# One-bank PSUM tiles, and loads ordered around DMA transposes, in an attention-and-mixer kernel

## The chip, the cores and the metric

The kernel runs on one core of one Trainium2 chip. The metric is device time in microseconds (us) of one execution. The profile also gives the span from the first to the last instruction.

## The reference, cut to what matters

```python
# q, k, v: [8 batches, 8 heads, 576 tokens, 64]; omega: [128, 64]
def phi(x):                       # random features, x scaled by 64 ** -0.25
    h = x @ omega.T - sum(x * x) / 2
    return exp(h - max(h)) / sqrt(128)
q_p, k_p = phi(q), phi(k)                  # [8, 8, 576, 128]
kv, z = k_p.T @ v, sum(k_p over tokens)    # per head
x = (q_p @ kv) / (q_p @ z + 1e-6)          # [8, 576, 512] over all heads
# token mixing, then channel mixing
u = x + (relu(x.T @ w_tok1) @ w_tok2).T    # 576 -> 256 -> 576
out = u + relu(u @ w_ch1) @ w_ch2          # 512 -> 1536 -> 512
```

What is constant in a token of q cancels in the division, so the kernel takes no maximum and no square sum for q. For k it divides by a maximum of the exponentials themselves, over the features of each token.

## The kernel before, in words

**Tiling.** Each batch b has 512 main tokens and a tail of 64; the tails of two batches share one 128-row tile. Attention goes by pairs of heads, `hp` = 0 to 3. Per pair: `kp` and `qp` multiply k and q, both with the head dimension on the partitions, by omega (lines 528 and 546); ACT takes the exponentials; DVE takes the maxima (`km`, line 558); Pool multiplies v by their reciprocals (`vs_`, line 567); `kv` (line 577) sums over the tokens; ACT copies it to SBUF; `num` (line 602) multiplies by the q features; DVE divides (`num_out`, lines 617 and 618) and writes x. The tails go through `kt`, `qt` and `vbd` first, once in a batch. Then token mixing (`token_mix`; the first batch in `token_mix_halves`) gives u, and channel mixing (`channel_mix`) gives the output: 48 matmuls on line 740 with a ReLU on ACT (line 746), 48 on line 755 and a sum on DVE (line 761). A ninth channel mixing (index B = 8) does all the tails, from `uTt`.

**How operands get their layout.** k and q of batches 0 and 1 are loaded with the tokens on the partitions and transposed on TensorE (`load_nat`, `transposes`, `tail_transposes`). For batches 2 to 7, `load_transposed` makes two steps per operand: a DMA from Pool casts fp32 to fp16 into a scratch in DRAM (line 335), and a DMA transpose from SP (line 341) brings it back as `qT` or `kT`. Pool then copies the tail's columns of `kT` to `ktt` (line 472). u of batches 1 to 7 is transposed into `uT` the same way from SP (line 659), and the tails' `ut` into `uTt` (line 729). SP also issues the stores and the loads of v's tails; Pool issues every load that casts, in one fixed order (`issued`).

**Order of work.** The order on each engine is planned ahead in Python. A job has an engine, an estimated cost, a key (smaller goes first), jobs that it depends on, buffers that it takes and buffers that it gives back. `Planner.run` picks, for each engine, the job that can start first by these estimates, ties by key. The instructions come out in that order and each engine runs its own list in order. The waits between engines are semaphores that the framework adds from which tile is read and written, so what really happens can differ from the estimates, and an instruction that waits holds up all behind it on its engine. While TensorE would be idle early on, `warm` puts in matmuls of zeros (line 799).

**PSUM.** It has eight banks, each 512 fp32 per partition. Before, they are four tiles of two banks:

```python
banks = [pspool.tile([P, 2, 512], FP32, name=f"bank{i}") for i in range(4)]
```

A job takes one bank (`width` 1) or an aligned pair (`width` 2: kt, qt, kp, qp, num). For single banks `find` has a preference: among those free by the estimates, one whose sibling in the same tile is in use goes first.

Of the kernel before, what the change touches and what calls it, by code (L numbers as in the profile page):

```python
# [26 lines left out]
class Planner:  # L27
# [25 lines left out]
    def find(self, tag, width=1):  # L53

        free = self.places[tag]
        best = None
        for i in range(0, len(free), width):
            at = max(free[i : i + width])
            tie = 0.0
            if width == 1 and tag == "bank":  # L60
                tie = -1.0 if free[i ^ 1] == math.inf else 0.0
            if at < math.inf and (best is None or (at > self.now, tie if at <= self.now else 0.0, at) < best[2]):
                best = (i, at, (at > self.now, tie if at <= self.now else 0.0, at))
        return best
# [3 lines left out]
    def run(self):  # L68
        at = {"PE": 0.0, "ACT": 0.0, "DVE": 0.0, "POOL": 0.0, "SP": 0.0}
# [5 lines left out]
        while any(waiting.values()):  # L75
            choice = None
            for eng, jobs in waiting.items():
                ready = []
                for j in jobs:
# [13 lines left out]
                    for tag, name, width in j.take:  # L93
                        if (tag, name) in self.held:
                            continue
                        got = self.find(tag, width)
                        if got is None:
                            ok = False
                            break
                        t = max(t, got[1])  # L100
# [30 lines left out]
            for tag, name, width in j.take:  # L131
                if (tag, name) in self.held:
                    continue
                i = self.find(tag, width)[0]
                for k in range(width):
                    self.places[tag][i + k] = math.inf
                self.held[tag, name] = (i, width)
# [13 lines left out]
            for g in j.give:  # L151
                self.left[g] -= 1
                self.freed[g] = max(self.freed.get(g, 0.0), j.end)
                if self.left[g] == 0:
                    i, width = self.held[g]
                    for k in range(width):
                        self.places[g[0]][i + k] = self.freed[g]
        return max(at.values())

    def place(self, tag, name):  # L160
        return self.held[tag, name][0]
# [3 lines left out]
def kernel(  # L165
# [12 lines left out]
    nc = tc.nc  # L178
# [27 lines left out]
    def ring(n, shape, dt, name):  # L206
# [3 lines left out]
             "kvsb": 3, "ktt": 2, "x": 3, "r1": 3, "u": 3, "uT": 3, "r3": 2, "o": 4, "bank": 8}  # L210
# [3 lines left out]
    banks = [pspool.tile([P, 2, 512], FP32, name=f"bank{i}") for i in range(4)]  # L214
# [3 lines left out]
    ident16 = sb([P, P], FP16, "ident16")  # L218
    zeros = sb([P, SM], FP16, "zeros")
# [38 lines left out]
    for b, t in ((0, t_r3[0]), (1, t_r3[1])):  # L258
        for i, w in enumerate("qk"):
            nat[w, b] = flat(t)[:, i * H * 256 : (i + 1) * H * 256].rearrange("p (h e) -> p h e", h=H)  # L260
        nat["t", b] = flat(t)[:, 2 * H * 256 : 2 * H * 256 + H * 2 * D].rearrange("p (h e) -> p h e", h=H)
# [7 lines left out]
    def bank(name):  # L269
        i = place("bank", name)  # L270
        return banks[i // 2][:, i % 2, :]
# [4 lines left out]
    def pair(name):  # L276
        return banks[place("bank", name) // 2]
# [20 lines left out]
    def load_nat(b, w, h0, h1, key, deps=()):  # L298
# [5 lines left out]
        job = dma("POOL", key, (h1 - h0) * 0.36, go, deps)  # L304
# [3 lines left out]
    def load_nat_tail(b, w, key, deps=()):  # L308
        o = 0 if w == "q" else RT
        def go():  # L310
            nc.gpsimd.dma_start(
                out=nat["t", b][o : o + RT], in_=src[w][b, :, SM:S, :].rearrange("h (r e) d -> r h (e d)", e=2)
            )
        ld[w + "t", b] = dma("POOL", key, 0.4, go, deps)

    def load_v(b, key, deps=(), h0=0, h1=H):
        def main():
            nc.gpsimd.dma_start(out=t_v[place("v", b)][:, h0:h1, :], in_=v[b, h0:h1, 0:SM, :].rearrange("h (p j) d -> p h (j d)", j=NJ))
        job = dma("POOL", key, 0.37 * (h1 - h0), main, deps, take=[("v", b, 1)], cost=0.5 + 0.05 * (h1 - h0))
# [3 lines left out]
    def load_v_tail(b, key, deps=()):  # L323
# [6 lines left out]
        ld["vt", b] = dma("SP", key, 0.5, tails, take=[("vt", b, 1)], deps=deps, cost=0.9)  # L330

    def load_transposed(b, key, deps=()):
        for n, w in enumerate("qk"):
            def cast(w=w):
# [3 lines left out]
                )  # L338
            def back(w=w):
                t = (t_qT if w == "q" else t_kT)[place(w + "T", b)]  # L340
                nc.sync.dma_start_transpose(out=t.unsqueeze(1), in_=scratch[w, b])
            c = dma("POOL", key + 0.01 * n, 2.9, cast, deps, cost=0.55)
            ld[w + "T", b] = dma("SP", key + 0.2 + 0.01 * n, 2.2, back, deps=[c], take=[(w + "T", b, 1)], cost=3.0)
# [11 lines left out]
    load_v_tail(0, -8.8)  # L355
    load_nat_tail(0, "k", -8.8)
    load_nat(0, "k", 4, 8, -8.7)
    load_nat_tail(0, "q", -8.6)
    load_nat(0, "q", 0, 4, -8.5)
    load_nat(0, "q", 4, 8, -8.4)  # L360
    load_v(0, -8.3, (), 0, 4)
    load_v(0, -8.2, (), 4, 8)

# [33 lines left out]
    for i in range(2):  # L397
# [7 lines left out]
                deps=[j_om16, j_ident], take=[("bank", "om", 1)])  # L405
# [9 lines left out]
    def transposes(b, w, h0, h1, key, on_act=False):  # L415
# [13 lines left out]
        take = [("bank", name, 1)]  # L429
        take.append((w + "T", b, 1))  # L430
# [5 lines left out]
    def tail_transposes(b, w, key):  # L436
        name, o = ("tt", b, w), 0 if w == "q" else RT
        def go():
            ps = bank16(name)
            for h in range(H):  # L440
                nc.tensor.transpose(ps[:, h * RT : (h + 1) * RT], nat["t", b][o : o + RT, h, :], ident16[o : o + RT, o : o + RT])
        def out_():
            ps = bank16(name)[:, 0 : H * RT].rearrange("p (h c) -> p h c", h=H)
            if w == "k":
                nc.vector.tensor_copy(out=t_ktt[place("ktt", b)].rearrange("p (h r) -> p h r", h=H), in_=ps)
            else:
                nc.vector.tensor_copy(out=rows_of(b, "q")[:, :, R:RA], in_=ps)
        t = add("PE", mm(8, 32), key, go, deps=[ld[w + "t", b], j_ident], take=[("bank", name, 1), ("ktt", b, 1) if w == "k" else ("qT", b, 1)], rows=True)
# [7 lines left out]
    def attention(b, key, step):  # L456
# [13 lines left out]
        if dma_in:  # L470
            def ktt():
                nc.gpsimd.tensor_copy(out=t_ktt[place("ktt", b)].rearrange("p (h r) -> p h r", h=H), in_=rows_of(b, "k")[:, :, R:RA])
            j_ktt = add("POOL", 0.5, key, ktt, deps=[ld["kT", b]], take=[("ktt", b, 1)], give=[("kT", b)])
# [7 lines left out]
        j_kt = add("PE", mm(2, P), key, kt, deps=[j_ktt, j_omT], take=[("bank", n_kt, 2), ("kpt", b, 1)], give=[("ktt", b)], rows=True)  # L481
        def kt_exp():
            exp(t_kpt[place("kpt", b)].rearrange("p g e m -> p e g m"), pair(n_kt)[:, :, 0 : 2 * M].rearrange("p e (g m) -> p e g m", g=2))
        j_kte = add("ACT", 0.5, key, kt_exp, deps=[j_kt], take=[("kpt", b, 1)], give=[("bank", n_kt)])
# [13 lines left out]
        j_ktm = add("DVE", 1.0, key + 0.01, kt_max, deps=[j_kte, j_mask], take=[("vbd", b, 1)])  # L498
# [16 lines left out]
        j_qt = add("PE", mm(1, 256), key + 0.1 * step, qt, deps=[src_of("q"), j_omT], take=[("bank", n_qt, 2), ("qpt", b, 1)], rows=True)  # L515
# [3 lines left out]
        j_qte = add("ACT", 0.5, key + 0.1 * step, qt_exp, deps=[j_qt, j_pads], take=[("qpt", b, 1)], give=[("bank", n_qt)])  # L519

        last_x = []
        for hp in range(NU):
# [5 lines left out]
            def kp(n_k=n_k, hh=hh):  # L528
                ps = pair(n_k)
                for i in range(2):  # L530
                    m = main("k", hh[i])
                    for r in range(2):
                        for e in range(2):
                            c = (2 * i + r) * M
                            nc.tensor.matmul(ps[:, e, c : c + M], m[half[e], r, :], omT[half[e]], start=True, stop=True)  # L535
            j_k = add("PE", mm(4, P), g, kp, deps=[src_of("k", hh[0]), src_of("k", hh[1]), j_omT], take=[("bank", n_k, 2), ("kp", (b, hp), 1)], rows=True,
# [4 lines left out]
            for e in range(2):  # L541
                def kp_exp(e=e, n_k=n_k, hp=hp):
                    exp(t_kp[place("kp", (b, hp))][:, :, e, :], pair(n_k)[:, e, :].rearrange("p (c m) -> p c m", c=4))
                je.append(add("ACT", 0.5, g, kp_exp, deps=[j_k], take=[("kp", (b, hp), 1)], give=[("bank", n_k)]))

            def qp(n_q=n_q, hp=hp):
                ps, t = pair(n_q), rows_of(b, "q")
                for e in range(2):
                    nc.tensor.matmul(ps[:, e, :], omT[half[e]], t[half[e], 2 * hp : 2 * hp + 2, 0:R], start=True, stop=True)  # L549
            j_q = add("PE", mm(1, 512), gq, qp, deps=[src_of("q", hh[0]), src_of("q", hh[1]), j_omT], take=[("bank", n_q, 2), ("qp", (b, hp), 1)], rows=True,  # L550
                      give=[("qT", b)])
            jq = []
            for e in range(2):
                def qp_exp(e=e, n_q=n_q, hp=hp):
                    exp(t_qp[place("qp", (b, hp))][:, e, :], pair(n_q)[:, e, :])
                jq.append(add("ACT", 0.5, gq, qp_exp, deps=[j_q], take=[("qp", (b, hp), 1)], give=[("bank", n_q)]))
# [8 lines left out]
            j_m = add("DVE", 1.42, g + 0.3 * step * (b > 0), km, deps=je, take=[("vs", (b, hp), 1)])  # L565
# [27 lines left out]
            j_kv = add("PE", mm(8, 65) + mm(2, 130), gv, kv, deps=[j_v, j_vbd, *je], take=[("bank", n_kv, 1), ("kvsb", (b, hp), 1)],  # L593
# [6 lines left out]
            j_kvo = add("ACT", 0.25, gv, kv_out, deps=[j_kv], take=[("kvsb", (b, hp), 1)], give=[("bank", n_kv)])  # L600
# [11 lines left out]
            j_n = add("PE", mm(10, 65), gv + 0.1 * step, num, deps=[j_kvo, j_qte, *jq], take=[("bank", n_n, 2), ("x", b, 1)],  # L612
# [11 lines left out]
            last_x.append(add("DVE", 1.04, gv + 0.1 * step, num_out, deps=[j_n], take=[("x", b, 1)], give=[("bank", n_n)]))  # L624
        return last_x, j_start

    def token_mix(b, key, step, jx):
        jr = []
        for tb in range(NT):
# [6 lines left out]
            j1 = add("PE", mm(5, 512), key + step * tb * 0.2, t1, deps=[*jx, j_w1, *j_w1t], take=[("bank", n, 1), ("r1", b, 1)])  # L636
            def relu(tb=tb, n=n):
# [3 lines left out]
                else:  # L641
                    nc.vector.tensor_relu(out=o, in_=bank(n))  # L642
            jr.append(add("ACT" if tb == 0 else "DVE", 0.5 if tb == 0 else 0.69, key + step * tb * 0.2, relu, deps=[j1],
                          take=[("r1", b, 1)], give=[("bank", n)]))
        ju = []
        for j in range(NJ):
# [5 lines left out]
            j2 = add("PE", mm(2, 512), key + step * (0.5 + 0.1 * j), t2, deps=[*jr, j_w2], take=[("bank", n, 1), ("u", b, 1)], give=[("r1", b)])  # L652
# [179 lines left out]
```

The softmax here doesn't subtract the row's maximum and nothing guards it: scores larger than these inputs give would overflow.

## Time and profile before

| What | Value |
|---|---|
| Times of three runs | 349.41, 357.22, 370.53 us |
| Median | 357.22 us |
| Profiled run | 348.81 us, span 347.1 us |
| Mean granted TensorE clock in it | 0.977 |
| PE (matmuls) busy | 296.5 us, 85% of the span |
| DVE, ACT, Pool busy | 148.3, 151.7, 79.9 us |
| Line 755, line 740 on PE | 105.0 us in 432 matmuls, 94.6 us in 384 |
| DMA | 39.58 MB, mean 114 GB/s |
| Queue that Pool feeds, queue that SP feeds | 32.9% and 30.7% of 16 engines' span |

The strips of the profile cut the span in 40 slices of 8.7 us; each digit is a busy share in tenths, and PEclk is the clock granted to TensorE in tenths of full speed. A wait line tells which engine and line waited, for which engine and line, then the total, the number of times and the longest, in us. A timeline line has start and length in us, engine, line, operation, what it writes and reads, how many are merged, and in brackets the idle time before it and what ended that. SPq is SP's queue: a DMA's line there lasts as long as issuing it holds the queue, not until the data has landed. Matmuls overlap in a pipeline, so the mean duration of one (383 ns for 512 columns) is longer than the 216 ns that one takes in a dense row.

### The profile page before, as it was taken

The numbers are of one execution on the slowest core, as the hardware profiler recorded it, in microseconds if no ns is written. First come the engines' busy times: TensorE is split into PE (matmuls) and PEld (weight loads), VectorE is DVE, ScalarE is ACT, GpSimd is POOL, SyncE is SP. The second block draws the span as 40 slices with busy tenths as digits, with TensorE's granted clock in tenths as the row PEclk, the third lists the DMA queues.
The fourth block names the chain that finished last, engine by engine and source line by source line (L and its number), as shares of the span: only waits on it lengthen the run. The fifth ranks groups of instructions, "written<-read, shape, count | busy, mean of one in ns | idle before, by whom it ended". The sixth has DMA issues, their size and how long they took to land.

```text
span 347.1 us, 5467 instructions
## 1 busy us (share of the span) xinstructions
PE 296.5 (85%) x2196; PEld 145.5 (42%) x2196; DVE 148.3 (43%) x302; ACT 151.7 (44%) x300; POOL 79.9 (23%) x92
## 2 busy tenths in 40 slices
PE   7788898089978968798889988989899979899993
PEld 3466354034534424344434433444344434344441
DVE  2874852228527552066345624563445323302011
ACT  1954872054654345425463456336643630150520
POOL 8692430015305170111330303021202100000000
PEclk9999999769999989999999999999999999999998
DMA  7999999993999999666694410411032003301104
GB/s 104 197 177 196 222 202 114 58 201 121 210 163 183 122 256 225 98 150 155 143 170 109 112 45 0 93 60 48 0 75 78 33 0 91 108 0 60 62 20 101
DMA packets 69849, 39.58 MB, mean 114 GB/s; under 512 B 47424, under 2 KB 64704, under 8 KB 69440
## 3 DMA queue, kind: packets, MB, share of 16 engines
q0 software_dynamic: 17408, 17.40, 32.9%
q1 hardware_dynamic: 52416, 21.83, 30.7%
q8 instruction: 17, 0.28, 0.3%
q14 instruction: 8, 0.07, 0.0%
HBM read 35.91 MB, written 16.52 MB: 151 GB/s over the span
## 4 chain that ended last, share of the span: by engine, by line
PE 59%; DMA 19%; DVE 11%; ACT 6%; issue 2%; POOL 2%; DVEq 0%; ACTq 0%
PE bank L740 24%; PE bank L755 22%; DMA qT<-q 7%; DMA q<-in_q_dram 5%; DMA uT<-u 4%; ACT r L746 3%; PE bank L634 3%; DVE u L654 3%; DMA wc<-in_moe_w_ch_dram 2%; PE bank L799 2%; DVE o L761 2%; PE bank L651 2%; DVE km L562 1%; POOL vs L569 1%; DVE mx L561 1%
## 5 line engine op out<-in xcount | busy, mean ns | idle before, releaser
L755 PE MATMUL bank<-wc,r 128*128 128x512 f16 x432 | 105.0, 383 | 9.8 <-DVE ut L727 3.7
L740 PE MATMUL bank<-uT,wc 128*128 128x512 f16 x384 | 94.6, 384 | 18.4 <-ACT r L746 9.3
L746 ACT ACTIVATE r<-bank 128x512 f16<-128x512 f32 x108 | 61.3, 600 | 96.2 <-PE bank L740 45.8
L740 PEld LDWEIGHTS <-wc 128*128 128x128 f16 x432 | 41.1, 98 | 65.4 <-issue 22.5
L755 PEld LDWEIGHTS <-r 128*128 128x128 f16 x432 | 40.7, 98 | 59.6 <-issue 18.1
L569 POOL TENSOR_TENSOR vs<-v,vs 128x512 f16<-128x512 f16 x32 | 34.1, 1070 | 108.5 <-DVE rc L617 53.3
L761 DVE TENSOR_TENSOR o<-u,bank 128x512 f32<-128x512 f16 x32 | 21.8, 685 | 56.4 <-PE bank L755 40.2
L452 ACT ACTIVATE kp<-bank 128x512 f16<-128x512 f32 x64 | 34.5, 610 | 20.9 <-PE bank L535 20.9
L452 ACT ACTIVATE qp<-bank 128x512 f16<-128x512 f32 x64 | 35.7, 628 | 14.0 <-PE bank L549 13.9
L618 DVE TENSOR_TENSOR x<-bank,rc 128x640 f16<-128x640 f32 x32 | 26.4, 824 | 1.1
L617 DVE RECIPROCAL rc<-bank 128x10 f32<-128x10 f32 x32 | 6.7, 208 | 43.9 <-PE bank L611 41.2
L596 ACT CAST kvsb<-bank 128x130 f16<-128x130 f32 x32 | 8.7, 283 | 35.7 <-DVE o L761 19.0
L654 DVE TENSOR_TENSOR u<-x,bank 128x512 f16<-128x512 f16 x28 | 17.9, 682 | 14.2 <-PE bank L651 11.8
L501 POOL TENSOR_TENSOR vbd<-vt,vbd 128x1024 f16<-128x1024 f32 x8 | 15.6, 1949 | 33.9 <-DVE vbd L492 33.9
L562 DVE TENSOR_REDUCE km<-mx 128x8 f16<-128x512 f16 x32 | 21.9, 686 | 1.1
L561 DVE TENSOR_TENSOR mx<-kp 128x512 f16<-128x512 f16 x32 | 17.1, 534 | 10.9 <-ACT kp L452 10.8
L549 PE MATMUL bank<-qT,omT 64*128 64x512 f16 x64 | 12.4, 386 | 10.2 <-DMA qT<-q 9.5
L582 PEld LDWEIGHTS <-kp 128*128 128x128 f16 x256 | 11.8, 98 | 8.8 <-issue 2.0
L609 PEld LDWEIGHTS <-qp 128*128 128x128 f16 x256 | 12.5, 98 | 6.4 <-issue 0.9
L634 PE MATMUL bank<-x,w1m 128*128 128x512 f16 x56 | 14.4, 379 | 0.0
L651 PE MATMUL bank<-r,w 128*128 128x512 f16 x56 | 14.4, 379 | 0.0
L642 DVE TENSOR_SCALAR r<-bank 128x512 f16<-128x512 f32 x7 | 4.8, 691 | 22.0 <-PE bank L740 11.8
(84 smaller groups left out, 249.1 us busy)
## 6 DMA issues: line engine op xcount, KB each, us to landing
out_dram<-o SPq DMA_DIRECT2D x32, 256.0 KB, 2.3
v<-in_v_dram POOLq DMA_DIRECT2D x7, 512.0 KB, 11.5
q<-in_q_dram POOLq DMA_DIRECT2D x6, 576.0 KB, 7.1
k<-in_k_dram POOLq DMA_DIRECT2D x6, 576.0 KB, 10.2
wc<-in_moe_w_ch_dram POOLq DMA_DIRECT2D x4, 768.0 KB, 13.9
vt<-in_v_dram SPq DMA_DIRECT2D x16, 64.0 KB
out_dram<-o SPq DMA_DIRECT2D x8, 128.0 KB, 2.3
r<-in_q_dram POOLq DMA_DIRECT2D x2, 256.0 KB, 6.7
```

Of the source, the lines that this page charges most:

```text
L452: nc.scalar.activation(out=out, in_=in_, func=AF.Exp, bias=0.0, scale=c_scale)
L561: nc.vector.tensor_tensor(out=tmp, in0=kpv[:, :, 0 : M // 2], in1=kpv[:, :, M // 2 : M], op=ALU.max)
L562: nc.vector.reduce_max(out=mx, in_=tmp, axis=AX.X)
L569: nc.gpsimd.tensor_tensor(out=vs[:, :, 0:D], in0=t_v[place("v", b)][:, hh[0] : hh[0] + 2, :].rearrange("p h (j d) -> p (h j) d", d=D), in1 ...
L618: nc.vector.tensor_tensor(out=t_x[place("x", b)][:, :, hp * 2 * D : (hp + 1) * 2 * D].rearrange("p j (i d) -> p i j d", i=2), in0=ps[:, :, ...
L634: nc.tensor.matmul(ps, w1m[:, j, tb * P : (tb + 1) * P], x[:, j, :], start=(j == 0), stop=False)
L651: nc.tensor.matmul(ps, w2[:, tb, 0:SM].rearrange("p (c j) -> p j c", j=NJ)[:, j, :], r1[:, tb, :], start=(tb == 0), stop=(tb == NT - 1))
L654: nc.vector.tensor_tensor(out=t_u[place("u", b)][:, j, :], in0=t_x[place("x", b)][:, j, :], in1=bank(n), op=ALU.add)
L740: nc.tensor.matmul(ps, wc1[:, db, cb * P : (cb + 1) * P], moving(db), start=(db == 0), stop=(db == ND - 1))
L746: nc.scalar.activation(out=t_r3[place("r3", c)][:, cb, :], in_=bank(n), func=AF.Relu)
L755: nc.tensor.matmul(ps, r3[:, cb, j * P : (j + 1) * P], wc2[:, cb, :], start=(cb == 0), stop=(cb == NCB - 1))
L761: nc.vector.tensor_tensor(out=t_o[place("o", (c, j))], in0=uu, in1=bank(n), op=ALU.add)
```

## The change

It has three parts, as its short description says: PSUM tiles of one bank instead of two; casts kept apart from DMA transposes by copies on Pool that read the transposes; tails in 4 KB rows.

- PSUM becomes six tiles of one bank and one tile of two. kp and qp take two single banks each and give each back by itself; kt, qt and num share the one pair. `find` has no preference for a sibling any more: of the banks free by the estimates it takes the one that has been free longest.
- The casts of q and k of a batch are queued one after the other, and each of the two transposes depends on both. The ktt copy moves into `load_transposed`; v of the batch depends on it. A new one-column copy on Pool, `touch`, reads the end of `uT` of batch b (1 to 5) into `junk`, and the casts of batch b + 2 depend on it. The old conditions (the start of attention of b - 2, and kT of the batch before) are gone.
- Tails of q and k of batches 0 and 1 are loaded with 16 tokens of a head in one partition's row (4 KB) in place of two (512 B), transposed in eight pieces as before, and put in order by the copy out of PSUM.
- At the start, k of heads 4 to 7 and q of heads 0 to 3 are queued ahead of the tails, and v's tail of batch 0 waits, by a small memset (`hold`), for k of heads 2 and 3. Some estimates of the planner are set anew.

```diff
-    def find(self, tag, width=1):
-        free = self.places[tag]
+    def find(self, tag, but=()):
         best = None
-        for i in range(0, len(free), width):
-            at = max(free[i : i + width])
-            tie = 0.0
-            if width == 1 and tag == "bank":
-                tie = -1.0 if free[i ^ 1] == math.inf else 0.0
-            if at < math.inf and (best is None or (at > self.now, tie if at <= self.now else 0.0, at) < best[2]):
-                best = (i, at, (at > self.now, tie if at <= self.now else 0.0, at))
+        for i, at in enumerate(self.places[tag]):
+            if at < math.inf and (tag, i) not in but and (best is None or (at > self.now, at) < best[2]):
+                best = (i, at, (at > self.now, at))
         return best
...
-        at = {"PE": 0.0, "ACT": 0.0, "DVE": 0.0, "POOL": 0.0, "SP": 0.0}
+        at = {"PE": 0.8, "ACT": 0.8, "DVE": 0.8, "POOL": 1.2, "SP": 0.7}
...
-             ... "bank": 8}
+             ... "bank": 6, "pair": 1}
-    banks = [pspool.tile([P, 2, 512], FP32, name=f"bank{i}") for i in range(4)]
+    banks = [pspool.tile([P, 512], FP32, name=f"bank{i}") for i in range(COUNT["bank"])]
+    pairs = [pspool.tile([P, 2, 512], FP32, name=f"pair{i}") for i in range(COUNT["pair"])]
...
-                out=nat["t", b][o : o + RT], in_=src[w][b, :, SM:S, :].rearrange("h (r e) d -> r h (e d)", e=2)
+                out=nat["t", b][o : o + RT].rearrange("p i e -> p (i e)"), in_=src[w][b, :, SM:S, :].rearrange("h (g f) d -> h g (f d)", g=4)
...
     def load_transposed(b, key, deps=()):
+        casts = []
         for n, w in enumerate("qk"):
             def cast(w=w):
...
+            casts.append(dma("POOL", key + 0.01 * n, 2.9, cast, deps, cost=0.55))
+        for n, w in enumerate("qk"):
             def back(w=w):
...
-            c = dma("POOL", key + 0.01 * n, 2.9, cast, deps, cost=0.55)
-            ld[w + "T", b] = dma("SP", key + 0.2 + 0.01 * n, 2.2, back, deps=[c], take=[(w + "T", b, 1)], cost=3.0)
+            ld[w + "T", b] = dma("SP", key + 0.2 + 0.01 * n, 2.2, back, deps=casts, take=[(w + "T", b)], cost=2.5)
+        def ktt():
+            nc.gpsimd.tensor_copy(out=t_ktt[place("ktt", b)]..., in_=t_kT[place("kT", b)]...[:, :, R:RA])
+        ld["ktt", b] = add("POOL", 0.4, key + 0.25, ktt, deps=[ld["kT", b]], take=[("ktt", b)], give=[("kT", b)])
+
+    def touch(b, key, uT):
+        def go():
+            nc.gpsimd.tensor_copy(out=junk[:, b : b + 1], in_=t_uT[place("uT", b)][:, NJ - 1, ND - 1, P - 1 : P])
+        return add("POOL", 0.15, key, go, deps=uT, give=[("uT", b)])
...
-    load_v_tail(0, -8.8)
-    load_nat_tail(0, "k", -8.8)
-    load_nat(0, "k", 4, 8, -8.7)
-    load_nat_tail(0, "q", -8.6)
-    load_nat(0, "q", 0, 4, -8.5)
+    load_nat(0, "k", 4, 8, -8.8)
+    load_nat_tail(0, "k", -8.7)
+    load_nat(0, "q", 0, 4, -8.6)
+    load_nat_tail(0, "q", -8.5)
     load_nat(0, "q", 4, 8, -8.4)
...
+    def hold():
+        nc.vector.memset(t_vt[place("vt", 0)][:, :, 0:1], 0.0)
+    load_v_tail(0, -8.8, [add("DVE", 0.1, -8.8, hold, deps=[ld["k", 0, 2]], take=[("vt", 0)])])
...
-            ps = bank16(name)[:, 0 : H * RT].rearrange("p (h c) -> p h c", h=H)
+            ps = bank16(name)[:, 0 : H * RT].rearrange("p (i h g) -> p i h g", i=8, h=H)
+            nc.vector.tensor_copy(out=to.rearrange("p h (g i) -> p i h g", g=4), in_=ps)
...
-                ps = pair(n_k)
+                ps = [bank((n_k, e)) for e in range(2)]
...
-            j_k = add("PE", mm(4, P), g, kp, ..., take=[("bank", n_k, 2), ("kp", (b, hp), 1)], ...)
+            j_k = add("PE", mm(4, P), g, kp, ..., take=[("bank", (n_k, 0)), ("bank", (n_k, 1)), ("kp", (b, hp))], ...)
...
-            j_n = add("PE", mm(10, 65), gv + 0.1 * step, num, ..., take=[("bank", n_n, 2), ("x", b, 1)],
+            j_n = add("PE", mm(10, 65), gv + 0.1 * step, num, ..., take=[("pair", n_n), ("x", b)],
...
-            load_transposed(b, b - 2.9, [started[b - 2], ld.get(("kT", b - 1))])
-            load_v(b, b - 2.6, [started[b - 2]])
+            load_transposed(b, b - 2.9, [touched.get(b - 2)])
+            load_v(b, b - 2.6, [ld["ktt", b]])
             load_v_tail(b, b - 2.0, [started[b - 1]])
...
+        if 0 < b < B - 2:
+            touched[b] = touch(b, b - 0.95, uT)
```

## The prediction, made before the change was run

> **What bounds the kernel now.** I read the 40-slice strip first, then who TensorE waits for, then the queues behind those waits.
>
> ```profile
> PE   7788898089978968798889988989899979899993
> PEclk9999999769999989999999999999999999999998
> DMA  7999999993999999666694410411032003301104
> ```
>
> A slice is 8.7 us. PE is near full but for one hole (slice 8, from 61 us), with a lowered clock in it. DMA is full up to 140 us, loose afterwards. So the limit is PE, with DMA behind it in the first third. PE is busy 296.5 of 347.1 us. Of the 50.6 idle, the stretches 0-32, 32-60 and 300-347 hold 6.0, 3.4 and 5.3; the rest lies between 60 and 300. The wait list of PE from 71 us (with the wait that began at 61) to 300 us names it (total, times, longest):
>
> ```profile
> PE bank L549 <- DMA qT<-q: 9.5, 1, 9.5
> PE bank L740 <- ACT r L746: 9.0, 16, 0.7
> PE bank L755 <- DVE ut L727: 3.7, 4, 1.5
> PE bank L740 <- DMA uT<-u: 3.0, 1, 3.0
> PE bank L755 <- DVE u L654: 2.4, 5, 1.0
> PE bank L755 <- DVE o L761: 2.1, 6, 0.4
> PE bank L740 <- DVE r L642: 1.8, 4, 0.8
> PE bank L740 <- ACT kvsb L596: 1.8, 4, 0.7
> ```
>
> Two families. Waits for a DMA transpose: 12.5 us. All others, with 2.5 us in rows not shown: 23.3 us. None of those can be a wait for data: L740 reads uT and weights, L755 reads r3, which ACT writes; DVE's u, o, ut are read by neither. They are waits for PSUM to be emptied.
>
> The first family, in the timeline of SP and of Pool (start, length):
>
> ```profile
> 47.72 16.89 SPq L341 DMA_TRANSPOSE qT<-q  x1
> 64.71 5.99 SPq L341 DMA_TRANSPOSE kT<-k  x1
> 70.76 1.96 SPq L659 DMA_TRANSPOSE uT<-u  x1
> ...
> 86.70 2.00 SPq L341 DMA_TRANSPOSE qT<-q  x1
> 88.80 2.92 SPq L341 DMA_TRANSPOSE kT<-k  x1
> ...
> 111.31 8.87 SPq L659 DMA_TRANSPOSE uT<-u  x1
> ```
>
> Pool's:
>
> ```profile
> 46.84 0.57 POOL L335 DMA_DIRECT2D q<-in_q_dram  x1
> 47.41 0.49 POOL L335 DMA_DIRECT2D k<-in_k_dram  x1
> ```
>
> The qT transpose of b=2 starts 0.9 us after Pool has queued the casts of b=3, and holds SP for 16.9 us; kT and the finished u of b=1 queue behind it. At 86.7, with no cast in flight, the same transposes hold SP 2.0 and 2.9. The uT of b=2 again meets two casts (110.6) and takes 8.9 us, 14.6 to landing.
>
> The second family shows where nothing but channel mixing runs:
>
> ```profile
> 302.65 1.08 ACT L746 ACTIVATE r<-bank 128x512 f16<-128x512 f32 x2 [0.41 <-PE bank L740]
> 304.38 1.08 ACT L746 ACTIVATE r<-bank 128x512 f16<-128x512 f32 x2 [0.64 <-PE bank L740]
> ```
>
> PE finishes a bank every 0.86 us, yet the ReLUs come in twos, every 1.73: the first of a tile waits until PE has filled the other half too. Here four tiles rotate and PE loses nothing. Beside attention fewer are free, and PE and ACT wait for each other in turn: at 167.53 ACT starts after 0.96 us idle, at 168.18 PE after 0.38 for that ReLU. I read it as a dependency kept per tile, not per bank; the old place finder makes it worse, since it prefers a bank whose sibling is in use.
>
> **What the Trainium skill says.** *Perfetto Trace Analysis*, Matmuls: independent groups should rotate through different PSUM banks so that emptying one overlaps filling the next. The paired ReLUs show the overlap lost. *PSUM — Partial Sum Buffer*, PSUM bank collisions: accesses need guarding per bank. So a wait covering two banks is the program's choice. *DMA: Bandwidth & Descriptors*, Rules for kernel authors: "A transpose next to ordinary DMAs needs nothing". That is about safety; for time this trace contradicts it (16.9 against 2.0 us). *TensorE: Matmul & The Clock Gate*, Part 1: idle lowers the clock. The trace agrees: 0.71 in 60-71 us, 0.90 over 71-90.
>
> **The change, part by part.**
>
> *Casts kept apart.* In Pool's DMA order b's v comes after the ktt copy, which reads kT, and the casts of b+1 come after v and after touch, which reads uT of b-1. For b=2 there is no touch. Its casts were issued at 28.6 and 31.3; q landed at 47.7 after 19 us behind the weights. That queue is bandwidth: 0.59 MB of q at 190 GB/s is 3.1 us, so k lands near 50.8. Both transposes now need both casts: start 50.8. Alone, as at 86.7, kT lands 7.3 us after qT's issue (ktt's wait ended at 94.0): qT near 55, kT near 58. Before, 70.8 and 72.8. PE stands ready at 61.3, so the **9.5 us hole goes**, and with it the slow clock after it: 10% of 19 us, **1.9**.
>
> v of b=2 is now issued at 58.5 instead of 34.0. A load alone takes about 8 us: 66.5. PE has 36 of the 48 L755 matmuls of c=0 left at 61.3, 7.8 us at 0.216, besides attention: hidden. uT of b=1 can go when u is done (62.9, plus 2 below): 65 plus 2.0 plus 2.3 landing is 69; PE needs it near 71. If it drags like the one at 111 (14.6), PE waits about 9 us; I keep that for the range.
>
> The uT of b=2 has no cast beside it: its **3.0 us** goes.
>
> Does the added wait bite? Behind touch on Pool stand the vs products; kv on PE waits for them, and PE is in order. From uT(b-2) landed: touch and issue 3, casts 10, transposes 8, v 9, attention 20 (four heads' pairs at about 2.4 us of DVE, with 10 lead-in), token mix and u 8, uT 4: 62 us for two batches. The old period is 35-36 a batch, hence 71; with the waits gone about 32.5, hence 65. It fits, narrowly. Copies: six ktt as before, five touches of at most 0.4 us (the ktt row is 398 ns for 256 columns): nothing, on an engine 23% busy.
>
> *One-bank tiles.* Six single tiles rotate, the longest free first; each ReLU starts after its own 0.86 us. Of 23.3 us the ceiling is all, the floor none (six in place of eight). ACT spends 0.6 per 0.86 of PE, so three banks keep L740 going and one L755; kp and qp take two each for about 1.3 us. That suffices most of the time. I take two thirds: **15 us**.
>
> *One pair.* num, kt and qt share it, so num of the next heads waits for DVE. In b=0 DVE ran the four outputs at 20.45, 21.46, 22.46, 23.44, spacing 1.0. Now each is followed by PE, about 0.6 plus 0.2 of signalling: 1.8 us spacing, 3 x 0.8 = 2.4 us later. The second half of token mix had 0.75 us of room (24.50 to 25.25): 1.7, **2 us lost** on the way to 61 us. Later the nums lie some 6 us apart and the 1.04 us output is done: nothing, with PE having L740 or L755 to put between.
>
> *Tails, v tail held, order of loads.* 4 KB rows put 32 rows where 256 of 512 B were, four times, beside a full DMA: at most 1 us, mostly hidden by DVE, which is the busy engine from 9.9 to 18.5. The scattered copy of 256 columns took 0.29 us; even doubled it is 4 x 0.3 under DMA waits. I take 0 for both.
>
> Sum: 347.1 - 9.5 - 1.9 - 3.0 - 15 + 2 = 319.7 us of span; the profiled run was 348.8 for 347.1, so add 1.7: about **322 us**. Cross-check from idle time: busy 294.6 (less the 1.9), idle 14.7 + 2 outside, 8.3 of bank waits left: 319.6. The median of before, 357.2, and its highest, 370.5, are more than this profile shows; such collisions may be what varies, which the change would also calm. I don't count on it.
>
> **The rivals.**
>
> *Only the transposes gain.* Six banks and one pair cost PE what the halves cost it. For: demand is high beside attention. Against: the waits come in PE-ACT pairs, the sign of a false dependency. 319.7 + 15 + 1.7 = **336**.
>
> *Only the banks gain.* The casts, now late, or v and uT overlapping, give back the 14.4 us elsewhere. For: DMA is full to 140 us and v loads are not kept apart. Against: volume is unchanged, and the mixed stretch moved under 80 GB/s. 319.7 + 14.4 + 1.7 = **336**.
>
> *All waits go.* 319.7 - 8 + 1.7 = **313**.
>
> *The chain of loads becomes the bound.* If casts, transposes and v take what the worst ones took (k 10, qT 23, v 11.5) the loop is 62 + 13 + 3 = 78, and with vs held behind touch a few more: 82, so 41 a batch against 35.4, over five batches +28. 347.1 - 9.5 + 2 + 28 + 1.7 = **369**, slower. Against: that 23 was collision, which the change forbids.
>
> **How the numbers follow.** Forecast 322: 55%. One half only (336, both ways): 26%. All (313): 9%. Loads as bound (369): 10%, with 7 of it over 2% slower and 3 within 2%; a further 2 within 2% I take from the halves, if both are partial. Range 311 to 344: below, the 313 case; above, 336 plus the 8 or so of a dragged uT. Faster means under 350.
>
> **What would show it.** No PE wait for qT<-q near 60 us, and every transpose on SP at 2 to 3 us (the casts' part). ReLUs one by one at 0.86 us in the last channel mixes, and PE's waits on ACT and DVE after 71 us at 8 us rather than 23 (the banks). Waits of the num matmuls for DVE's output only in b=0 (the pair). Wrong would be: PE waiting for vs or kT in b=3 to 5, SP transposes still at 6 us or more, or bank waits over 15 us.

## The result, and the profile after

The changed kernel takes **305.94 us** (median of four runs, 305.1 to 307.0) against 353.32 us before (345.3 to 370.5): a ratio of **0.8806, 95% interval 0.873 to 0.8882**. (Some executions fall into a slower state, and the ratio leaves those out: it sets the four of the changed kernel against the two faster ones of the kernel before, 345.32 and 349.41 us.) The span of the profiled run falls from 347.1 to 304.7 us. Faster was right, but the gain is larger than the forecast of 322 us; the measured time lies under the low end of my range, 311.

Lines 740, 746, 755, 617 and 618 of before are 744, 750, 759, 621 and 622 here. The strips of the changed kernel's page, 40 slices of 7.6 us:

```profile
PE   8749989999999999999999999999999999999992
PEclk9997999999999999999999999999999999999998
DMA  6999999876898797599856697897651015103023
```

PE has no hole any more; its one weak spot before the end is in slice 3, about 15 to 23 us, and the clock is down in slice 4. DMA is full up to 53 us only, no longer up to 140, and then at half or more up to about 230. The wait list of PE over the whole span, its first rows (total, times, longest in us):

```profile
PE bank L586 <- POOL vs L573: 3.7, 1, 3.7
PE pair L613 <- DVE x L622: 1.2, 3, 0.9
PE bank L805 <- DVE mask L375: 1.2, 1, 1.2
```

All rows together are 9.5 us in 11 waits, against 44.1 us in 62 before. The whole list from 71 us on is one row, 0.9 us, where before it was 35.8 us in 45 waits:

```profile
PE pair L613 <- DVE x L622: 0.9, 1, 0.9
```

Both families are gone from there on: nothing waits for the DMA of qT or uT, and nothing for a single bank that ACT or DVE has still to empty. The row that is left is num waiting for DVE to empty the one pair. The other 8.6 us lie in the first 71 us.

ACT's timeline in the last but one channel mixing (start, length, in brackets the idle time before and its releaser) answers to the paired ReLUs of before:

```profile
259.66 0.60 ACT L750 ACTIVATE r<-bank 128x512 f16<-128x512 f32 x1 [0.27 <-PE bank L744]
260.52 0.60 ACT L750 ACTIVATE r<-bank 128x512 f16<-128x512 f32 x1 [0.27 <-PE bank L744]
261.39 0.60 ACT L750 ACTIVATE r<-bank 128x512 f16<-128x512 f32 x1 [0.27 <-PE bank L744]
```

One ReLU every 0.86 us, each right after its own bank. SP's timeline around the transposes of b=2 and b=3:

```profile
49.12 4.08 SPq L338 DMA_TRANSPOSE qT<-q  x1
53.30 2.47 SPq L338 DMA_TRANSPOSE kT<-k  x1
...
70.04 1.38 SPq L663 DMA_TRANSPOSE uT<-u  x1
...
82.23 3.62 SPq L338 DMA_TRANSPOSE qT<-q  x1
85.94 3.23 SPq L338 DMA_TRANSPOSE kT<-k  x1
```

What took 16.9 and 6.0 us at 47.7 now takes 4.1 and 2.5 at 49.1.

### The profile page after: what moved, and what is told of

It is laid out like the page before. It is cut to its first block, busy times and chain, and to the rows that moved or that the text cites. A ratio compares the mean times of both kernels' runs of the same rounds, so it can differ in the third digit from the quotient of the medians.

```text
span 304.7 us, 5507 instructions
## 1 busy us (share of the span) xinstructions
PE 289.5 (95%) x2206; PEld 144.1 (47%) x2206; DVE 147.9 (49%) x303; ACT 154.5 (51%) x300; POOL 80.7 (26%) x97
## 4 chain that ended last, share of the span: by engine, by line
PE 87%; DVE 5%; DMA 4%; issue 1%; POOL 1%; ACT 0%; SPq 0%; DVEq 0%; POOLq 0%
PE bank L759 31%; PE bank L744 29%; PE bank L655 4%; PE bank L638 4%; DMA vt<-in_v_dram 4%; PE pair L613 3%; PE bank L805 3%; PE bank L539 3%; PE bank L586 2%; PE bank L553 2%; PE bank L593 1%; PE bank L725 1%; DVE x L622 1%; PE bank L639 1%; DVE km L566 1%
## 5 line engine op out<-in xcount | busy, mean ns | idle before, releaser
L759 PE MATMUL bank<-wc,r 128*128 128x512 f16 x432 | 102.9, 379 | 0.0
L750 ACT ACTIVATE r<-bank 128x512 f16<-128x512 f32 x108 | 64.2, 605 | 65.3 <-PE bank L744 65.2
L744 PE MATMUL bank<-uT,wc 128*128 128x512 f16 x384 | 90.6, 379 | 0.0
L759 PEld LDWEIGHTS <-r 128*128 128x128 f16 x432 | 40.0, 98 | 45.5 <-issue 2.3
L744 PEld LDWEIGHTS <-wc 128*128 128x128 f16 x432 | 40.0, 98 | 45.2 <-issue 2.5
L458 ACT ACTIVATE kp<-bank 128x512 f16<-128x512 f32 x64 | 34.5, 611 | 16.4 <-PE bank L539 16.3
L458 ACT ACTIVATE qp<-bank 128x512 f16<-128x512 f32 x64 | 34.8, 615 | 15.3 <-PE bank L553 15.2
L621 DVE RECIPROCAL rc<-pair 128x10 f32<-128x10 f32 x32 | 6.6, 207 | 44.4 <-PE pair L615 44.3
L622 DVE TENSOR_TENSOR x<-pair,rc 128x640 f16<-128x640 f32 x32 | 26.4, 824 | 1.1
L658 DVE TENSOR_TENSOR u<-x,bank 128x512 f16<-128x512 f16 x28 | 18.0, 680 | 11.1 <-PE bank L655 11.0
L586 PE MATMUL bank<-vs,kp 128*128 128x65 f16 x256 | 13.6, 197 | 3.7 <-POOL vs L573 3.7
L805 PE MATMUL bank<-zeros 128*128 128x512 f16 x43 | 14.6, 459 | 1.4 <-DVE mask L375 1.2
L613 PE MATMUL pair<-kvsb,qp 128*128 128x65 f16 x256 | 14.3, 195 | 1.3 <-DVE x L622 1.2
```

The source lines that it names most:

```text
L458: nc.scalar.activation(out=out, in_=in_, func=AF.Exp, bias=0.0, scale=c_scale)
L586: nc.tensor.matmul(ps[:, i, :], kpv[:, 2 * i + j // 2, j % 2, :], vs[:, i * NJ + j, 0 : D + 1], start=(i == 0 and j == 0), stop=False, ski ...
L613: nc.tensor.matmul(ps[:, i, j * 65 : (j + 1) * 65], st, s[:, i, 0 : D + 1], start=True, stop=True)
L622: nc.vector.tensor_tensor(out=t_x[place("x", b)][:, :, hp * 2 * D : (hp + 1) * 2 * D].rearrange("p j (i d) -> p i j d", i=2), in0=ps[:, :, ...
L744: nc.tensor.matmul(ps, wc1[:, db, cb * P : (cb + 1) * P], moving(db), start=(db == 0), stop=(db == ND - 1))
L750: nc.scalar.activation(out=t_r3[place("r3", c)][:, cb, :], in_=bank(n), func=AF.Relu)
```

## The experiments

All times are medians; the kernel before, run beside them, had medians of 349 to 350 us. The planner makes a new order after most edits. TensorE's order of matmuls is the changed kernel's in experiment 1 alone, and the two kernels of experiment 6 share one; in every other comparison with the changed kernel or the one before, a new order is part of what is measured.

**1. Is the dependency kept per tile?** Only the declaration of the six single banks changes. The order of TensorE's instructions and the bank that each uses stay as they were.

```diff
-    banks = [pspool.tile([P, 512], FP32, name=f"bank{i}") for i in range(COUNT["bank"])]
+    banks = [t[:, i, :] for t in [pspool.tile([P, 2, 512], FP32, ...) for n in range(COUNT["bank"] // 2)] for i in range(2)]
```

> The changed kernel with its six single banks declared as three tiles of two banks; the order of instructions on every engine and the bank of every matmul stay the same. Theory 1 (a dependency is kept per tile, so emptying one bank waits for filling the other): PE waits on ACT and DVE come back, 20 us or more after 71 us, ReLUs pair up again at 1.7 us where both banks of a tile follow each other; 325 to 340 us. Theory 2 (the gain came from the new order and the place finder, the longest free bank first): no such waits, 304 to 308 us.

Measured: **340.39 us** (338.96 to 342.12), 34.5 above the changed kernel and just over theory 1's range. PE's waits are 30.5 us in 51, against 9.5 in 11; 14.7 us of them lie after 71 us, less than the 20 that I wrote for that part, and none is for a DMA or Pool. PE's busy time is 300.5 against 289.5 us. The first rows of this kernel's wait list of PE from 71 us on:

```profile
PE bank L759 <- ACT qp L458: 1.5, 2, 1.2
PE bank L655 <- DVE u L658: 1.3, 3, 0.7
PE bank L744 <- ACT qp L458: 1.2, 1, 1.2
PE bank L655 <- ACT kp L458: 1.2, 1, 1.2
```

Its timeline of ACT in a channel mixing near the end:

```profile
295.69 0.60 ACT L750 ACTIVATE r<-bank 128x512 f16<-128x512 f32 x1 [0.27 <-PE bank L744]
297.42 1.57 ACT L750 ACTIVATE r<-bank 128x512 f16<-128x512 f32 x3 [1.13 <-PE bank L744]
299.14 0.60 ACT L750 ACTIVATE r<-bank 128x512 f16<-128x512 f32 x1 [0.15 <-PE bank L744]
```

A channel mixing's second layer (L759) has nothing to do with the features qp that ACT is emptying; what they can share is a tile. ACT sits idle for 1.13 us with one finished bank, then does three in a row. Theory 1 holds, and theory 2 falls: with the same order on PE, the sharing of tiles alone is worth the 34.5 us.

Not all of that is steady loss. Set against the same matmul of the changed kernel, this one is 12.2 us behind at 71 us and 32.5 at the end. In the first part the clock takes a share: between 20 and 30 us it is granted at 0.50 here, at 0.79 to 0.86 in the changed kernel.

**2. What does the finder's preference for a sibling do, in the kernel before?**

```diff
-                tie = -1.0 if free[i ^ 1] == math.inf else 0.0
+                tie = 0.0
```

> The kernel before without the finder's preference for a bank whose sibling is in use. Theory 1 (dependency per tile): neighbours are still shared, so most of the 23 us of PSUM waits stays; 340 to 352 us. Theory 2 (the preference made the waits): they fall below 8 us; 320 to 332 us.

Measured: **335.16 us** (334.04 to 336.71; a fourth run took 339.12). Neither number was right. PE's waits from 71 us are 26.3 us; 9.9 of it is still the qT wait and 6.6 one for Pool, so some 10 us of PSUM waits are left of 23.3. With the preference, which puts neighbours in use next to each other, more than half of that kernel's PSUM waits go. How much of this is the preference itself and how much the new order of TensorE is not told apart. Experiment 1 has no such preference and still loses 34.5 us, so a shared tile is enough for the loss, and the preference at most an amplifier.

**3. The loads alone**: the kernel before with the new conditions for casts, transposes, ktt, touch and v.

```diff
-            load_transposed(b, b - 2.9, [started[b - 2], ld.get(("kT", b - 1))])
-            load_v(b, b - 2.6, [started[b - 2]])
+            load_transposed(b, b - 2.9, [touched.get(b - 2)])
+            load_v(b, b - 2.6, [ld["ktt", b]])
...
```

> The kernel before with the new conditions of casts, transposes, ktt, touch and v only; PSUM tiles, finder, start and tails as before. Theory (the parts add): the qT wait of 9.5 us and the uT wait of 3 us are gone, the PSUM waits stay near 23 us; 332 to 340 us. Rival (a later batch of loads bounds it): 345 us or more.

Measured: **335.77 us**, 0.9605 of before (0.9554 to 0.9655). Its wait list of PE from 71 us:

```profile
PE bank L751 <- ACT r L757: 8.5, 16, 0.7
PE bank L751 <- ACT r L651: 3.4, 5, 0.7
PE bank L766 <- DVE ut L738: 2.3, 2, 1.5
```

No row for a DMA is left there. 22.6 us of waits stay, 1.6 of them for Pool's products and nearly all others for banks, of which the kernel before had 23.3 (L751, L757 and L766 are its L740, L746 and L755). Its four runs lie within 0.8 us, where seven of the kernel before spread over 4.4.

**4. The banks alone, in two steps.** First the old conditions of the loads in the changed kernel:

```diff
-            load_transposed(b, b - 2.9, [touched.get(b - 2)])
-            load_v(b, b - 2.6, [ld["ktt", b]])
+            load_transposed(b, b - 2.9, [started[b - 2], ld.get(("kT", b - 1))])
+            load_v(b, b - 2.6, [started[b - 2]])
...
-            ld[w + "T", b] = dma("SP", ..., deps=casts, ...)
+            ld[w + "T", b] = dma("SP", ..., deps=[casts[n]], ...)
```

> The changed kernel with the old conditions of casts, transposes and v (start of attention of b - 2, kT of the batch before, no touch, v early, each transpose after its own cast). Theory 1 (the parts add): the qT wait near 60 us is back at 8 to 12 us and SP transposes of 6 us and more too; 318 to 326 us. Rival A (with a faster PE the transposes bound every batch): over 330 us. Rival B (the loads' part was hidden, the banks did it all): under 310 us.

Measured: **310.63 us** (309.72 to 311.17), between theory 1 and rival B. There is no wait for qT, only 2.4 us for one uT, though the transposes do collide: qT of b=4 holds SP for 8.62 us. Pool's order gave a reason. The ktt copy, which I had left where the change puts it, stands ahead of the next casts and waits for kT by a semaphore. The condition `ld["kT", b - 1]` does not: it exists in the planner alone. So the second step puts ktt back into attention, and the old place and estimate of the transposes with it.

> As banks_only, and the ktt copy is put back into attention with its old key and estimate, so that nothing on Pool keeps the casts of b=3 behind the transposes of b=2. Theory (that copy is what removed the hole in banks_only, since it waits for kT by a semaphore and the casts stand behind it on Pool): casts of b=3 go out before the qT of b=2 starts, the wait for qT near 60 us is back with 5 us or more; 314 to 324 us. Rival (the one-bank order on PE alone hides it): 309 to 312 us, as banks_only.

Measured: **313.89 us** (311.88 to 314.3). This kernel's timeline of Pool around the transposes of b=2:

```profile
54.87 0.56 POOL L330 DMA_DIRECT2D q<-in_q_dram  x1
55.42 0.50 POOL L330 DMA_DIRECT2D k<-in_k_dram  x1
66.82 0.39 POOL L473 COPY ktt<-kT 128x256 f16<-128x256 f16 x1 [10.90 <-DMA kT<-k]
```

The same stretch on SP:

```profile
50.39 5.79 SPq L336 DMA_TRANSPOSE qT<-q  x1
56.29 8.44 SPq L336 DMA_TRANSPOSE kT<-k  x1
```

The casts of b=3 do get ahead of ktt again, and kT is slow for it (8.44 us), but they come 4.5 us after the start of qT, where before they came 0.9 us ahead, and PE waits only 1.9 us, for kT. The expected qT wait of 5 us did not return; the time lies at the low end, 314. So the size of the hole hangs on a few microseconds of timing: 9.5 us with the casts 0.9 us ahead of qT, 1.9 us with them 4.5 us behind its start.

So the four corners are 350 (neither), 336 (loads), 314 (banks with the new start and tails) and 306 us (both). Loads bring 14.5 alone and 8 beside the banks; the parts overlap.

**5. Which condition of the loads counts?** Without touch:

```diff
-            load_transposed(b, b - 2.9, [touched.get(b - 2)])
+            load_transposed(b, b - 2.9, [started[b - 2]])
```

> The changed kernel without touch: casts of b may go out at the planned start of attention of b - 2, behind v and ktt on Pool as before. Theory 1 (touch only keeps uT apart from the casts, and uT has room): single uT transposes of 5 to 9 us on SP, hardly a wait on PE; 304 to 308 us. Theory 2 (touch is needed): PE waits for uT by 3 us or more; 309 us or more.

Measured: **309.24 us** (308.61 to 309.85): theory 2's time without theory 2's wait. One uT takes 7.39 us on SP, the others 1.8 to 3.4, and PE never waits for one. What grew is the wait of num for DVE, 3.5 us against 1.2. TensorE's order is another one without touch, so I can't say that keeping uT from the casts is what touch brings; that stays open. And v no longer behind ktt:

```diff
-            load_v(b, b - 2.6, [ld["ktt", b]])
+            load_v(b, b - 2.6, [started[b - 2]])
```

> The changed kernel with v of a batch queued right behind its casts again, no longer behind the ktt copy, so that v's cast runs beside the qT transpose. Theory 1 (any cast beside a transpose slows it, but there is room): qT on SP at 5 us or more in place of 3.4 to 4.1, and no wait on PE for it; 304 to 307 us. Theory 2 (v beside the transposes is what the room can't take): PE waits for kT, qT or vs by 3 us or more; 309 us or more.

Measured: **307.38 us** (305.06 to 309.08), not clearly other than the changed kernel. SP, for the same two batches as above:

```profile
50.56 5.75 SPq L338 DMA_TRANSPOSE qT<-q  x1
56.41 3.34 SPq L338 DMA_TRANSPOSE kT<-k  x1
...
83.76 6.01 SPq L338 DMA_TRANSPOSE qT<-q  x1
89.86 4.07 SPq L338 DMA_TRANSPOSE kT<-k  x1
```

With v's cast beside it as well, every qT takes 5.75 to 8.72 us, where the changed kernel has 2.44 to 4.08 for the same six; PE waits 0.7 us in all for the transposes. Slower transposes are real, and mostly hidden.

**6. The start.** v's tail of batch 0 without the hold:

```diff
-    load_v_tail(0, -8.8, [add("DVE", 0.1, -8.8, hold, deps=[ld["k", 0, 2]], take=[("vt", 0)])])
+    load_v_tail(0, -8.8)
```

> The changed kernel with v's tail of batch 0 loaded at the very start again, without the memset that holds it back. Theory 1 (the held tail landed at 19.8 us instead of under 14 and is what delayed batch 0): the vbd on Pool starts by 16 us and the whole is 3 to 5 us faster, 301 to 303 us. Rival (DMA is full then, so something else of the start comes late instead): 305 to 307 us.

Measured: **304.34 us** (303.72 to 304.91), between the two expectations. Pool's vbd in the timeline of the changed kernel:

```profile
19.81 1.93 POOL L505 TENSOR_TENSOR vbd<-vt,vbd 128x1024 f16<-128x1024 f32 x1 [5.40 <-DMA vt<-in_v_dram]
```

And in this one:

```profile
14.83 1.93 POOL L503 TENSOR_TENSOR vbd<-vt,vbd 128x1024 f16<-128x1024 f32 x1 [0.27 <-DVE vbd L494]
```

The held tail comes 5 us late, and the weak spot of PE's strip in slice 3 (digit 4) goes with the hold: the digit is 7 here, though slice 5 falls from 9 to 6. Only 1.6 us reaches the end. Then the tails in 512 B rows again and the plain copies, both at once:

```diff
-            ps = bank16(name)[:, 0 : H * RT].rearrange("p (i h g) -> p i h g", i=8, h=H)
-            nc.vector.tensor_copy(out=to.rearrange("p h (g i) -> p i h g", g=4), in_=ps)
+            ps = bank16(name)[:, 0 : H * RT].rearrange("p (h c) -> p h c", h=H)
+            nc.vector.tensor_copy(out=to, in_=ps)
```

> As no_hold, with the tails of q and k in rows of 512 B again and the plain copies out of PSUM. Theory (the scattered copies cost 1.24 us of DVE each instead of 0.29, and that weighs more than the shorter rows): the copies take 0.3 us and the first matmuls of channel mixing come 1 to 2 us earlier; 302 to 303.5 us. Rival (short rows slow the loads of the start by as much or more): 304 to 306 us.

Measured: **302.99 us** (302.87 to 303.11). The copy of 256 columns in the timeline of DVE of the changed kernel:

```profile
11.04 1.24 DVE L453 COPY ktt<-bank 128x256 f16<-128x256 f16 x1
```

And in this one:

```profile
10.97 0.29 DVE L451 COPY ktt<-bank 128x256 f16<-128x256 f16 x1 [0.33 <-PE bank L447]
```

**7. How many singles?**

```diff
-             ... "bank": 6, "pair": 1}
+             ... "bank": 4, "pair": 2}
```

> The changed kernel with two pairs and four single banks in place of one pair and six. Theory 1 (the single pair costs the start: outputs of b=0 spaced 1.65 us; four singles are too few later): the outputs of b=0 come every 1.0 us, up to 2 us won there, and PE gets PSUM waits or lost density of 5 us and more after 60 us; 306 to 315 us. Theory 2 (singles are plentiful, the pair is what is short): 303 to 305 us.

Measured: **317.04 us** (316.88 to 318.0; a fourth run took 321.9). The last outputs of b=0 do come every 1.0 us (25.26, 26.26, 27.24), and 11.1 us are lost all the same. About half of them are idle time: between 60 and 268 us PE waits 6.2 us in 9 waits, where the changed kernel has 0.9 from 71 us to its end. 3.1 us of it are waits for a bank to be emptied, 2.4 one wait for Pool's products. PE's busy time is longer too, 294.8 us against 289.5, with a granted clock of 0.978 against 0.991. The single pair is the cheaper choice, and the upper bound I wrote was too low. That four singles run short explains the bank waits; how much of the rest is theirs and how much the new order's is not shown.

**8. Is the better version real?** The changed kernel and no_hold_old_tails once more, side by side on one chip.

> The changed kernel once more, on the same chip as the next one, so that the two can be set side by side: 305 to 307 us.

> no_hold_old_tails once more: if what the hold and the scattered copies cost is real, 302.5 to 303.5 us on this chip too, 2 us or more under the changed kernel beside it; if it was the chip or the call, the two are within 1 us.

Measured: 305.65 us (304.59 to 306.45) and **302.97 us** (302.69 to 303.28). The ranges don't meet: 2.7 us. The version without hold and with plain tails is faster than both kernels of this case, 0.8709 of before (0.8666 to 0.8753).

## Why the prediction was right, and where it was not

*What bounds it, and the first family.* Right. The waits for qT and uT (9.5 and 3.0 us) are gone, and loads_only, which removes them alone, gains 14.5 us where the step said 14.4. What I did not see is that this sum can't be added to the banks': beside them the loads bring 8 us, because there the casts of b=3 go out at 54.9 us, not 46.8, and the DMA wait is down to 1.9 us anyway (banks_only_full).

*The single terms of that step.* qT and kT of b=2 landing near 55 and 58 us: Pool's wait for kT ended at 59.3. "Both transposes now need both casts" was wrong, as is "each of the two transposes depends on both" in the account of the change: that stands in the plan, but the transposes read different scratches, and no semaphore came of it. In the changed kernel q of b=2 lands at 49.10 us and qT starts at 49.12, while k lands at 52.85. So a batch's own k cast still runs beside its qT, and "every transpose on SP at 2 to 3 us" was too low: qT takes 3.4 to 4.1 us in the five batches where k lands at least 1.4 us after its start, 2.44 in the one where k lands 0.2 us after it, and 2.00 in my model row of before, where no cast was in flight. Other DMAs differ between these too, so this is an observation and no test. PE waits for none of them.

*One-bank tiles, 15 us.* This is the term that was mis-sized. Its mechanism is shown by experiment 1. Its size, beside the loads and with the new start in it, is 29.8 us (loads_only to the changed kernel), where the forecast had 15 less 2 for the pair. Two things were wrong. I took two thirds of 23.3 us of waits, and 22.4 of it went: six singles, the longest free first, leave no wait for one after 71 us. And I took the idle time for the whole cost. PE's busy time fell as well, from 296.5 to 289.5 us, of which I had counted 1.9 for the clock. loads_only settles that part: its clock is 0.995, nearly all its bank waits are still there, and its busy time is 294.7. So 1.8 us go with the loads and 5.2 with the banks. A group of four matmuls spans 1.02 us before a wait (at 85.3 us in the kernel before) and 0.86 in a dense row; 0.16 us for each of the 51 waits that went is 8, which is of the right size, but is arithmetic and not an experiment.

*One pair, 2 us lost.* The spacing is as worked out (1.65 us against 1.8), yet the start has other costs that I had set to zero: the held tail (1.6 us, with a new order in it) and the tails in 4 KB rows (1.3 us for rows and copies together, in which each scattered copy takes 1.24 us, four times the 0.29 that I had allowed to double). Side by side the two are 2.7 us, in experiment 8. "Nothing" for the hold failed because I looked at what the load of the tail would free, and not at when it lands in a full queue. Idle time before 60 us is 9.0 us, not the 11.4 that the forecast implies, but that is no gain in work: 43 matmuls of zeros fill 14.6 us of PE there, against 33 and 11.2 before, and the 400th matmul of real work starts at 51.7 us, against 48.6.

*Does the added wait bite.* Right: the loop of loads fits. Casts of b=3 go at 76.7, transposes at 82.2, v at 91.7, and PE shows no wait for vs after b=0. v of b=2 landed 6.1 us after its issue, where I had put 8.

The sum then reads: span 319.7 forecast, 304.7 measured; 7.4 us from the waits for banks, 5.1 from busy time, 2.4 from idle time before 60 us, 0.1 left over; the zeros move some of that between the last two. Of the rivals, "all waits go" came nearest, and even it left out the busy time. The two "one half only" cases were both wrong as forecasts: 336 is what the loads alone give, but the banks alone give 314. In the loads as a bound I mis-added: transposes of 23 us in place of 8 make 15, not 13, so that its loop would have been near 80, not 78.

## What to carry to other kernels

When an engine empties buffers in twos while it is offered them one by one, look for a dependency that covers more than the buffer: experiment 1 changed a declaration and nothing else for 34.5 us. Many short waits can cost more than their idle time: here PE's busy time fell by 5.2 us with them. A dependency in a plan orders nothing by itself: read in the trace whether the wait is there, as it is not between k's cast and qT. Keeping DMAs apart pays where a queue stands in line behind the slow one, so price it by what waits there, and expect it to overlap with every other change that moves the timing.

## What the runs showed of the hardware that was not expected

- The scattered copy out of PSUM writes single 2-byte elements eight apart: 1.24 us and more for 256 columns, 0.29 with dense runs. The Trainium skill (*VectorE: DVE Perf Modes*, What auto-detection actually checks) names a step of one among the conditions of the faster modes; the trace agrees in direction, and its factor is over 4.
- In no_hold_old_tails one DVE maximum over SBUF, 0.42 us in the median of 32, takes 3.91 us (15.12 to 19.03) while Pool multiplies, also out of SBUF, from 14.78 to 18.73; in the second run of the same kernel it is 3.86. *SBUF — State Buffer*, SBUF: two separate sides, says that a DVE instruction with two SBUF inputs and a GpSimd one that reads SBUF exclude each other. The times fit that, though why DVE got no turn between Pool's three instructions is open; no run here was made to test it.
